# Decay attention with a SoLU layer on one core: GpSimd centres z by adding the negated mean, and the order of all operations is searched anew

## The chip, the cores and the metric

The kernel runs on one core of a Trainium2 chip. The metric is the device time of one execution in microseconds (us); lower is better. A core has five engines that run side by side, each working through its own instructions in order: TensorE (PE in the profile, its weight loads PEld), VectorE (DVE), ScalarE (ACT), GpSimd (POOL) and SyncE (SP), which issues the DMAs here. They wait for one another on semaphores.

## The reference, cut to what matters

```python
# attention: q, k, v (8, 8, 576, 64), f (8, 8, 576)
scores = scale * np.matmul(q, k.transpose(0, 1, 3, 2))
cum = np.cumsum(np.log(np.clip(f, 0.0001, 1.0)), axis=-1)
scores = np.where(causal, -1000000000.0, scores + cum[:, :, :, None] - cum[:, :, None, :])
attn = np.exp(scores - max(scores)) ; attn = attn / (sum(attn) + 1e-09)
x = (attn @ v)  # as 4608 tokens x 512
# layer: w_in (512, 1024), w_out (1024, 512)
h = x @ w_in
e = np.exp(h - h_max)
solu = h * e / (np.sum(e, axis=-1, keepdims=True) + 1e-09)
mu = np.mean(solu, axis=-1, keepdims=True)
var = np.mean((solu - mu) ** 2, axis=-1, keepdims=True)
ln = (solu - mu) / np.sqrt(var + 1e-06) * g_ln
return ln @ w_out
```

The last lines are what the change touches: each token's 1024 values are centred by their mean and scaled by their deviation before the second product.

## The kernel before, in words

Every fp32 operand of a product is split into a high and a low fp16 part, and each product is three fp16 matmuls (high x high, low x high, high x low). The kernel works in two interleaved streams.

*Attention.* 32 pairs of heads (8 batches x 4 pairs). For a pair, `split_qk` and `split_v` make the fp16 parts: GpSimd the high part (L489, L750), VectorE the low one (L741, L751). `score_products` (TensorE, L778 and L780) fills PSUM banks, VectorE masks and takes the maximum (L800), ScalarE takes the exponential (L805), GpSimd adds 1e-9 to the sums (L811) and VectorE inverts them (L812). P is scaled and split into fp16 by ScalarE or GpSimd (L487, L489) and VectorE (L827), transposed by DMA on SP's queue (L496), and multiplied by v (TensorE, L849); ScalarE and VectorE split the result into x (L858, L859).

*Layers.* 36 groups of 128 tokens, `layer(n)`. TensorE makes h in PSUM (L879 to L881). VectorE takes its maximum (L892, L893), ScalarE the exponential (L895), VectorE weighs it by h and sums (L899). GpSimd turns the sums into factors: `sums` (L903 to L905), where L905 makes `s[:, 4:5]`, the mean. ScalarE squares and sums the deviations (L909), and GpSimd's `deviation` (L913, L914) makes `s[:, 7:8]`, the reciprocal deviation. Then z is made from `et`, which holds the weighed values:

- for layers 3 to 32 (30 of them), L919 on GpSimd centres `et` in place, with mean and deviation as operands taken per partition; ScalarE copies it to fp16 (L487, tile z), GpSimd subtracts to get the low part (L923), and both are transposed by one DMA;
- for layers 0 to 2, 33 and 34, L928 on GpSimd writes the centred z in fp32, and TensorE transposes it (L939), with splits by ScalarE (L942) and VectorE (L943);
- for layer 35, L928 runs on VectorE in two halves.

TensorE makes the output of the layer in a PSUM bank (L951 to L953), ScalarE scales it (L983) and SP stores it.

The order of the work is made by a planner when the program is built. Every operation is entered with an engine, a cost in ns, its dependences, and a rank from the list `RANK` (3720 entries), which takes the place of the due time given with it. `Plan.schedule` then simulates the five engines by those costs and takes, on each engine, the lowest rank among the operations that are ready or nearly so. What comes out is a fixed order of instructions per engine (SP's DMA queue included) and the PSUM bank of each product. On the chip each engine keeps this order, whatever the real durations are. The planner's costs that matter here: 1165 ns for the centring at L919 and 1220 at L928 on GpSimd, 650 for `deviation`, 950 for `sums`, 1350 for the weighing, and 150 (`SWITCH`) whenever TensorE goes from one form of matmul to another. Where the planner sees TensorE idle before 140 us and after 690 us of its own time, it puts matmuls on a constant (L1075) that compute nothing.

Of the kernel before, what the change touches and what calls it, by code (L numbers as in the profile page):

```python
# [15 lines left out]
ALU = mybir.AluOpType  # L16
# [3 lines left out]
B, H, S, D = 8, 8, 576, 64  # L20
NPAIR = H // 2
NT, DM, DFF = B * S, 512, 1024
# [15 lines left out]
PE, ACT, DVE, POOL, SP = range(5)  # L38
# [23 lines left out]
SWITCH = ((0.0, 150.0, 0.0, 150.0), (150.0, 0.0, 150.0, 150.0), (0.0, 150.0, 0.0, 150.0), (150.0, 150.0, 150.0, 0.0))  # L62
# [11 lines left out]
class Plan:  # L74
# [125 lines left out]
DUE = dict(split=16.32, v=-48.52, S=((10.42, -178.61), (-76.5, -43.51), (-17.84, 9.11), (-33.83, -25.65), (-338.51, -196.13)), T=(109.24, 340.52, -82.29, -127.23, -60.67), V=(-7.63, 56.62))  # L200
EARLY = dict(split=362.28, v=-97.59, S=((-411.23, -149.52), (-71.89, 66.22), (-245.09, -190.59), (-76.46, 23.88), (22.21, -234.26)), T=(-72.02, -152.54, -5.6, -408.25, -113.91), V=(-252.88, -30.84))
LATE = dict(split=98.43, v=174.22, S=((-17.11, -184.22), (262.31, 198.88), (-309.42, 7.37), (-32.81, 315.39), (118.17, -135.55)), T=(-189.94, -447.79, -346.65, 143.53, -213.83), V=(45.44, 171.68))
PAIR = 19.22
C_OUT = -1186.29
C_LOAD = -414.2
START = 55.12
HALF = ((-18.23, 31.03), (-177.88, -65.59))
FINAL = ((612.38, -120.01), (574.97, -91.39))
W_IN = (-124.17, -35.6)
W_OUT = (114.81, 6.76)  # L210
WI_SCALE = (-281.95, 282.86)
VDUE = (271.75, 1385.66, -57.91)
QDUE = (148.6, 265.36, 191.09)
W_SCALE = 469.26
W_DMA = (340.69, 250.23)
AT_P = ((-81.67, 61.16, 60.23, 192.14, 69.55, -100.01, -98.02, 300.72), (-145.79, 357.44, 17.6, 61.32, 14.21, -14.54, -172.11, 33.3), (141.14, 169.03, -125.66, -194.75, -29.29, 69.66, -241.42, -50.24), (-161.17, 125.62, -280.73, -119.52, -307.95, 75.0, -172.56, 168.03), (53.4, 12.94, 59.05, -81.54, -65.95, -187.09, -104.95, -79.9), (57.9, 109.17, -65.96, 150.72, -25.16, -82.81, 36.45, -8.16), (70.77, 133.63, 12.76, -7.44, 191.47, -123.42, 272.56, -18.37), (21.29, 142.9, 37.73, 313.97, 43.82, -67.44, 60.97, -521.28), (174.0, 168.03, 225.82, 361.17, 52.24, 81.8, 314.01, -241.37), (74.44, -51.03, 294.31, 305.07, 2.7, 84.27, -129.0, -33.77), (119.59, -15.83, -61.33, 18.64, -123.18, -57.85, 111.65, -131.16), (68.91, -122.6, 34.58, -83.09, 83.91, 102.57, -179.31, 35.06), (190.89, 62.67, 9.66, 34.42, -143.48, -186.72, -16.07, -334.64), (15.13, -57.55, -54.74, -107.42, -116.07, -287.16, -220.22, -252.55), (332.62, -121.34, -54.52, -218.21, -55.32, -30.68, 22.54, 170.65), (-57.32, -255.01, -70.11, -225.0, -2.07, 17.04, -35.42, -47.88), (-27.85, 64.37, -177.02, -84.25, -204.85, 158.78, 40.98, -78.34), (64.44, 76.4, -166.26, -216.1, 128.23, 164.74, 20.38, -202.94), (-67.41, -175.96, -53.63, -139.42, -116.31, 92.32, -98.02, 23.06), (-34.62, -99.73, -34.72, -107.59, -43.28, 25.95, -59.91, 21.41), (-197.38, 99.1, 77.91, -87.49, -101.39, -44.62, -10.73, -432.6), (76.35, -52.66, -146.11, -57.9, -32.02, 20.35, -9.36, -41.36), (284.63, -33.64, -59.72, -35.36, 13.16, -50.56, 111.1, -209.08), (-170.21, 17.59, 22.48, -18.35, -145.72, 148.72, -38.82, -153.28), (117.16, -118.25, -147.0, -84.5, -216.07, -97.89, 17.93, -21.37), (19.52, 129.07, 84.34, 107.44, 28.14, 165.39, 116.59, -105.27), (35.5, 2.96, -74.65, -119.02, -111.77, 33.07, -159.25, 73.15), (-137.99, -76.09, 98.87, -83.71, 39.3, 53.58, 88.01, 118.53), (-73.29, -23.24, -279.13, -8.79, 152.09, -154.48, -73.79, 73.15), (116.11, 4.31, -44.41, 87.07, -47.65, 327.91, 111.04, 63.74), (119.79, 166.23, -85.34, -98.88, -1.08, 185.35, -23.71, 210.62), (-10.74, 3.74, 66.08, 111.57, -99.16, -276.89, -13.72, -336.84))
STEPS = (-4.08, -26.31, -34.38, -3.27, -7.29)
XSTEP = (-40.34, 35.34)
AT_L = ((-254.45, -131.81, -28.71, 162.54), (129.2, 133.0, -66.4, -97.75), (0.16, 51.2, -66.64, -216.93), (27.84, 199.95, 50.97, 33.36), (-31.05, -140.35, 257.32, 37.01), (9.35, -73.92, -30.24, -139.45), (75.8, 16.59, 6.38, -28.89), (-31.5, -16.15, 5.27, 35.3), (-99.98, -146.39, -116.22, -14.35), (-0.39, -65.93, -16.48, 55.16), (36.33, -12.74, -45.85, 6.72), (-41.24, -55.87, -46.44, 40.3), (7.03, 41.84, -82.9, -173.0), (-93.41, -117.32, -38.75, -26.07), (-47.53, 52.85, 15.16, -87.73), (10.27, 20.72, 230.99, 138.02), (10.21, 46.78, 185.1, 145.78), (56.68, -116.87, -221.71, 140.0), (85.62, -125.98, -15.49, 39.67), (-161.28, 65.64, -134.56, -113.34), (28.35, 25.51, -55.67, 64.12), (-33.19, -41.91, 47.28, -41.75), (-92.58, 111.35, 0.14, 39.65), (-45.33, 21.88, 91.63, 134.69), (228.29, -26.11, -19.26, -117.38), (-117.29, 36.02, -120.02, 67.48), (237.85, 58.15, -36.94, -123.12), (-185.8, -87.16, -219.01, 97.21), (42.34, 163.22, 98.63, 248.34), (-34.9, -42.96, 198.6, -38.06), (203.64, 142.69, 74.54, -92.81), (-202.74, 75.26, -28.07, -252.01), (-86.6, -144.99, 45.93, 151.88), (218.16, 25.2, 97.92, 313.38), (308.03, -15.23, -72.11, -87.35), (3.75, -320.4, 375.02, -12.8))
FIRST = 89.94  # L220
STAGES = (62.88, 1.27, -19.84, 26.95, 22.69)

RANK = (
# [151 lines left out]
def tile_kernel(ctx: ExitStack, tc: tile.TileContext, qk, v, f, w_in, w_out, g_ln, out):  # L375
# [104 lines left out]
    def engine(e):  # L480
        return {DVE: nc.vector, POOL: nc.gpsimd}[e]
# [640 lines left out]
```

## Time and profile before

| what | value |
|---|---|
| median of 3 runs | 766.3 us (763.89 to 771.79) |
| profiled execution | 766.7 us, span 764.7 us |
| granted TensorE clock, mean | 0.971 |
| centring on GpSimd (L919), 30 passes | 115.7 us, 3787 ns median |
| the same to fp32 z (L928), 5 passes | 19.0 us, 3787 ns median |
| low part of z (L923), 30 passes | 64.8 us, 2130 ns median |

Rows of the profile name a line of the kernel, an engine, and tiles as output<-inputs with their shapes. Numbers such as 3781/3787/4849 are the least, the median and the greatest duration in ns, followed by the start of the first and the last one in us. A row of waits reads "waiting instruction <- what it waited for: us in total, times, longest us". In a row of order in time, a bracket at the end gives the engine's idle time before the instruction and what ended it.

### The profile page before, as it was taken

What the parts mean: (1) busy time and instruction counts of PE and PEld (TensorE: products, weight loads), DVE (VectorE), ACT (ScalarE), POOL (GpSimd) and SP (SyncE); (2) the same over time, 40 slices, a digit from 0 to 9 for tenths busy, and PEclk for the clock granted to TensorE, in tenths of its full rate; (3) what the DMA queues carried; (4) which work ended last, traced back from release to release, by engine and by line L of the source; (5) the groups of instructions that cost most, each with busy time, mean ns of one, the idle gap of its engine ahead of it and who ended that gap; (6) DMA issues with size and microseconds to landing.
All of it is one profiled execution on the core that took longest, in us unless ns stands there. A gap on an engine that the chain in (4) does not pass through costs nothing. (4 is left out here: it accounts for less than half of the span.)

```text
span 764.7 us, 18744 instructions
## 1 busy us (share of the span) xinstructions
PE 684.8 (90%) x6937; PEld 389.3 (51%) x6937; DVE 577.5 (76%) x1701; ACT 533.8 (70%) x1334; POOL 460.1 (60%) x599
## 2 busy tenths in 40 slices
PE   9999987885979998997899898998898997979998
PEld 8877654543444444444444454444454544445445
DVE  4798888987886988778878787997888865575422
ACT  7788947778777876776667776987767667553433
POOL 4330386456269467587388776787587585373750
PEclk9999999997889999999999999999999999998999
DMA  8699157867957798997779866998494577458321
GB/s 355 232 257 196 41 90 192 153 172 154 197 139 158 162 177 171 178 158 140 152 121 225 166 130 140 216 180 174 108 162 108 119 114 134 77 111 144 82 55 42
DMA packets 284241, 116.33 MB, mean 152 GB/s; under 512 B 269814, under 2 KB 270262, under 8 KB 283126
## 3 DMA queue, kind: packets, MB, share of 16 engines
q1 hardware_dynamic: 284150, 115.14, 70.8%
q8 instruction: 54, 0.88, 0.5%
q14 instruction: 37, 0.30, 0.1%
HBM read 38.12 MB, written 9.88 MB: 63 GB/s over the span
## 5 line engine op out<-in xcount | busy, mean ns | idle before, releaser
L805 ACT ACTIVATE ps<-ps,nm 128x192 f32<-128x192 f32 (+3 forms) x256 | 113.8, 445 | 32.8 <-DVE nm L800 29.6
L780 PE MATMUL ps<-qk 64*128 64x288 f16 (+4 forms) x1152 | 98.1, 281 | 25.6 <-DVE wo_p L827 12.2
L919 POOL TENSOR_SCALAR e<-e,st 128x1024 f32<-128x1024 f32 x30 | 115.7, 3857 | 2.9
L951 PE MATMUL ps<-wo_f,zz 128*128 128x512 f16 x280 | 107.7, 385 | 10.8 <-DVE p16s L827 4.7
L849 PE MATMUL ps<-t_p,v 128*64 128x128 f16 (+1 forms) x2880 | 98.6, 226 | 21.0 <-DVE p16s L827 10.0
L879 PE MATMUL hps<-wi_h,x_h 128*128 128x512 f16 x288 | 111.5, 387 | 5.7 <-DVE e L899 5.7
L811 POOL TENSOR_SCALAR sm<-sm 128x2 f32<-128x2 f32 (+1 forms) x128 | 38.4, 300 | 126.7 <-ACT ps L805 97.8
L800 DVE CUSTOM_DVE_ANT_0 ps<-ps,mask 128x192 f32<-128x192 f32 (+3 forms) x256 | 102.9, 444 | 11.1 <-PE ps L778 10.6
L880 PE MATMUL hps<-wi_l,x_h 128*128 128x512 f16 x288 | 111.1, 386 | 0.0
L881 PE MATMUL hps<-wi_h,x_l 128*128 128x512 f16 x288 | 110.7, 384 | 0.0
L849 PEld LDWEIGHTS <-v 128*64 128x64 f16 x2880 | 87.2, 115 | 43.0 <-issue 39.2
L952 PE MATMUL ps<-wo_f,zz 128*128 128x512 f16 x280 | 107.2, 383 | 0.0
L953 PE MATMUL ps<-wo_f,zz 128*128 128x512 f16 x280 | 106.9, 382 | 0.0
L487 ACT ACTIVATE p16s<-ps,ri 64x64 f16<-64x64 f32 (+2 forms) x192 | 68.8, 416 | 19.4 <-DVE ri L812 17.2
L827 DVE SCALAR_TENSOR_TENSOR p16s<-ps,ri,p16s 128x192 f16<-128x192 f32 (+2 forms) x192 | 71.2, 406 | 14.3 <-ACT p16s L487 13.5
L780 PEld LDWEIGHTS <-qk 64*128 64x128 f16 x1152 | 44.9, 95 | 68.0 <-issue 52.5
L923 POOL TENSOR_TENSOR z<-e,z 128x1024 f16<-128x1024 f32 x30 | 64.8, 2161 | 17.4 <-ACT z L487 16.8
L487 ACT ACTIVATE z<-e 128x1024 f16<-128x1024 f32 x30 | 31.7, 1057 | 60.8 <-POOL e L919 60.7
L1075 PEld LDWEIGHTS <-ident 128*128 128x128 bf16 x673 | 65.0, 99 | 14.6 <-issue 4.5
L1075 PE MATMUL hps<-ident 128*128 128x256 bf16 x560 | 65.9, 277 | 1.3 <-POOL ident masks.py:199 1.3
L741 DVE SCALAR_TENSOR_TENSOR qk<-raws,scale,qk 128x576 f16<-128x576 f32 x64 | 58.0, 917 | 8.6 <-POOL qk L489 8.4
L489 POOL TENSOR_SCALAR qk<-raws,scale 128x576 f16<-128x576 f32 x64 | 50.0, 790 | 21.6 <-DVE scale L638 9.0
(171 smaller groups left out, 1348.2 us busy)
## 6 DMA issues: line engine op xcount, KB each, us to landing
raws<-in_qk_dram SPq DMA_DIRECT2D x32, 576.0 KB, 7.0
vraw<-in_v_dram SPq DMA_DIRECT2D x8, 1280.0 KB
out_dram<-y SPq DMA_DIRECT2D x35, 256.0 KB, 3.5
wo_raw<-in_w_in_dram SPq DMA_DIRECT2D x4, 1024.0 KB
vraw<-in_w_out_dram SPq DMA_DIRECT2D x2, 1024.0 KB, 6.7
t_raw<-in_w_out_dram SPq DMA_DIRECT2D x2, 1024.0 KB, 7.7
t_p<-p16s SPq DMA_TRANSPOSE x96, 3.2
t_p<-wo_p SPq DMA_TRANSPOSE x64, 5.3
```

The costliest lines, as they stand in the source:

```text
L780: nc.tensor.matmul(dst, x[row(h), 0, q0:q0 + P], y[row(h), 1, cols], start=(n == 0), stop=False)
L800: op(DVE, R_NS[i] if n == 0 else 442, at[i][h] + STEPS[0], lambda i=i, h=h, n=n, a=a, e=e, x=x, m0=m0: nc.vector.tensor_tensor_reduce(home ...
L805: op(ACT, E_NS[i], at[i][h] + STEPS[1], lambda i=i, h=h, x=x: nc.scalar.activation(home(i, h), home(i, h), AF.Exp, bias=x, scale=-1.0, acc ...
L849: nc.tensor.matmul(o[row(h), a:a + n], v16[m][:, x, 2 * j + h], t[:, y, i + j if h else i - j], start=(j == 0 and c == 0), stop=(j == i an ...
L879: nc.tensor.matmul(hps[:, sl], x_h, wi_h[:, c, sl], start=(c == 0), stop=False)
L880: nc.tensor.matmul(hps[:, sl], x_h, wi_l[:, c, sl], start=False, stop=False)
L881: nc.tensor.matmul(hps[:, sl], x_l, wi_h[:, c, sl], start=False, stop=(c == NCC - 1))
L919: op(c_eng, {POOL: 1165, DVE: 690}[c_eng], at, lambda: engine(c_eng).tensor_scalar(et, et, s[:, 4:5], s[:, 7:8], ALU.subtract, ALU.mult), ...
L951: nc.tensor.matmul(o, zz[:, a, 0, j], wo(0, k), start=(k == 0), stop=False)
L952: nc.tensor.matmul(o, zz[:, a, 0, j], wo(1, k), start=False, stop=False)
L953: nc.tensor.matmul(o, zz[:, a, 1, j], wo(0, k), start=False, stop=(k == NFC - 1))
L1075: nc.tensor.matmul(dst[:, :256], blank[:, :P], blank, start=True, stop=True)
```

## The change

The mean is stored with a negative sign, and the centring adds it in place of subtracting it, in all three places:

```diff
-            nc.gpsimd.tensor_scalar(s[:, 4:5], s[:, 3:4], 1.0 / DFF, 1.0, ALU.mult, ALU.mult)
+            nc.gpsimd.tensor_scalar(s[:, 4:5], s[:, 3:4], -1.0 / DFF, 1.0, ALU.mult, ALU.mult)
...
-            op(c_eng, {POOL: 1165, DVE: 690}[c_eng], at, lambda: engine(c_eng).tensor_scalar(et, et, s[:, 4:5], s[:, 7:8], ALU.subtract, ALU.mult),
+            op(c_eng, {POOL: 1165, DVE: 690}[c_eng], at, lambda: engine(c_eng).tensor_scalar(et, et, s[:, 4:5], s[:, 7:8], ALU.add, ALU.mult),
...
-                    zt[:, sl], et[:, sl], s[:, 4:5], s[:, 7:8], ALU.subtract, ALU.mult), [ek, ("st4", n % 2), ("st7", n % 2)], [zk], clear=[zk_, (*zk_, "l")], port=c_eng == DVE)
+                    zt[:, sl], et[:, sl], s[:, 4:5], s[:, 7:8], ALU.add, ALU.mult), [ek, ("st4", n % 2), ("st7", n % 2)], [zk], clear=[zk_, (*zk_, "l")], port=c_eng == DVE)
```

Three of the planner's costs change, those of the centring stay:

```diff
-SWITCH = ((0.0, 150.0, 0.0, 150.0), (150.0, 0.0, 150.0, 150.0), (0.0, 150.0, 0.0, 150.0), (150.0, 150.0, 150.0, 0.0))
+SWITCH = ((0.0, 120.0, 0.0, 120.0), (120.0, 0.0, 120.0, 120.0), (0.0, 120.0, 0.0, 120.0), (120.0, 120.0, 120.0, 0.0))
...
-        op(DVE, 1350, at, weigh, [("h",)], [("st3", n % 2), ek])
+        op(DVE, 1220, at, weigh, [("h",)], [("st3", n % 2), ek])
...
-        op(POOL, 650, at, deviation, [("st5", n % 2), ("st4", n % 2)], [("st7", n % 2)])
+        op(POOL, 1030, at, deviation, [("st5", n % 2), ("st4", n % 2)], [("st7", n % 2)])
```

All entries of `RANK` are new: the same 3720 ranks, dealt out again. Half of the operations move by 12 places or fewer, the one that moves most by 248. The tables of due times (`DUE`, `EARLY`, `LATE`, `AT_P`, `AT_L` and the constants beside them) change too; the rank takes their place in the planner.

More of the change, by code (lines that the diff above doesn't have):

```diff
@@ L196, in spare @@
                 a = min(y for spans in self.held.values() for _, y in spans if y > a)
-DUE = dict(split=16.32, v=-48.52, S=((10.42, -178.61), (-76.5, -43.51), (-17.84, 9.11), (-33.83, -25.65), (-338.51, -196.13)), T=(109.24, 340.52, -82.29, -127.23, -60.67), V=(-7.63, 56.62))
-EARLY = dict(split=362.28, v=-97.59, S=((-411.23, -149.52), (-71.89, 66.22), (-245.09, -190.59), (-76.46, 23.88), (22.21, -234.26)), T=(-72.02, -152.54, -5.6, -408.25, -113.91), V=(-252.88, -30.84))
-LATE = dict(split=98.43, v=174.22, S=((-17.11, -184.22), (262.31, 198.88), (-309.42, 7.37), (-32.81, 315.39), (118.17, -135.55)), T=(-189.94, -447.79, -346.65, 143.53, -213.83), V=(45.44, 171.68))
@@ L203 @@
[L203 to L216, printed above, removed]
@@ L217 @@
-STEPS = (-4.08, -26.31, -34.38, -3.27, -7.29)
-XSTEP = (-40.34, 35.34)
-AT_L = ((-254.45, -131.81, -28.71, 162.54), (129.2, 133.0, -66.4, -97.75), (0.16, 51.2, -66.64, -216.93), (27.84, 199.95, 50.97, 33.36), (-31.05, -140.35, 257.32, 37.01), (9.35, -73.92, -30.24, -139.45), (75.8, 16.59, 6.38, -28.89), (-31.5, -16.15, 5.27, 35.3), (-99.98, -146.39, -116.22, -14.35), (-0.39, -65.93, -16.48, 55.16), (36.33, -12.74, -45.85, 6.72), (-41.24, -55.87, -46.44, 40.3), (7.03, 41.84, -82.9, -173.0), (-93.41, -117.32, -38.75, -26.07), (-47.53, 52.85, 15.16, -87.73), (10.27, 20.72, 230.99, 138.02), (10.21, 46.78, 185.1, 145.78), (56.68, -116.87, -221.71, 140.0), (85.62, -125.98, -15.49, 39.67), (-161.28, 65.64, -134.56, -113.34), (28.35, 25.51, -55.67, 64.12), (-33.19, -41.91, 47.28, -41.75), (-92.58, 111.35, 0.14, 39.65), (-45.33, 21.88, 91.63, 134.69), (228.29, -26.11, -19.26, -117.38), (-117.29, 36.02, -120.02, 67.48), (237.85, 58.15, -36.94, -123.12), (-185.8, -87.16, -219.01, 97.21), (42.34, 163.22, 98.63, 248.34), (-34.9, -42.96, 198.6, -38.06), (203.64, 142.69, 74.54, -92.81), (-202.74, 75.26, -28.07, -252.01), (-86.6, -144.99, 45.93, 151.88), (218.16, 25.2, 97.92, 313.38), (308.03, -15.23, -72.11, -87.35), (3.75, -320.4, 375.02, -12.8))
@@ L220 @@
-FIRST = 89.94
-STAGES = (62.88, 1.27, -19.84, 26.95, 22.69)
-RANK = (
[148 rows of a table removed]
+DUE = dict(split=26.66, v=-44.32, S=((17.02, -148.33), (-64.42, -44.95), (-28.43, 12.9), (-42.71, -39.48), (-325.28, -188.8)), T=(64.32, 327.76, -59.68, -127.5, -47.39), V=(-7.74, 31.59))
+EARLY = dict(split=332.95, v=-57.66, S=((-372.38, -152.17), (-57.66, 30.21), (-183.97, -159.95), (-60.8, 76.81), (-22.89, -163.49)), T=(-33.47, -7.72, -4.8, -396.65, -124.51), V=(-142.51, -66.42))
+LATE = dict(split=81.6, v=174.09, S=((-5.61, -234.66), (198.9, 135.47), (-236.01, 0.28), (28.81, 328.08), (107.14, -163.85)), T=(-115.44, -433.88, -336.19, 140.0, -108.98), V=(-5.0, 176.08))
@@ new lines @@
+PAIR = 18.5
+C_OUT = -1212.08
+C_LOAD = -650.15
+START = 54.54
+HALF = ((53.14, -17.86), (-150.28, -79.69))
+FINAL = ((625.5, -127.51), (555.3, -109.92))
+W_IN = (-77.74, 17.6)
+W_OUT = (120.75, 49.66)
+WI_SCALE = (-540.34, 296.98)
+VDUE = (387.16, 1315.13, -62.36)
+QDUE = (217.4, 372.26, 220.19)
+W_SCALE = 360.35
+W_DMA = (193.38, 344.79)
+AT_P = ((25.12, 95.62, 42.16, 214.24, 43.75, -38.59, -81.69, 295.75), (-140.06, 200.42, -1.28, 29.81, 26.59, -27.74, -186.97, 33.02), (151.37, 195.04, -155.18, -161.83, -33.15, 38.49, -268.94, -41.72), (-188.64, 177.31, -240.94, -78.79, -249.47, 134.65, -191.84, 84.33), (78.5, -23.93, -9.71, -105.86, -48.06, -187.29, -125.06, -49.3), (-10.91, 90.41, -28.2, 131.1, -90.03, -116.36, 52.65, -32.0), (44.39, 170.77, 20.96, 2.3, 190.15, -182.08, 257.81, -7.06), (-32.76, 95.23, 28.91, 293.82, 41.19, 24.48, 59.59, -494.43), (127.94, 195.94, 193.63, 316.21, 45.94, 34.03, 326.37, -137.96), (-6.2, -97.44, 217.38, 248.58, 19.46, 70.9, -92.14, -25.49), (121.42, 60.05, -22.1, -11.23, -121.91, -2.29, 132.03, -111.33), (32.66, -138.46, 79.08, -42.76, 99.42, 117.62, -152.76, 38.35), (196.54, 55.31, -3.46, 61.33, -136.97, -285.2, 55.2, -274.07), (-45.42, -1.66, -57.0, -59.94, -99.97, -248.68, -156.0, -313.23), (386.4, -82.49, -41.1, -212.17, -144.74, -39.5, 22.85, 130.81), (-59.36, -348.05, -101.26, -223.62, 19.02, 26.31, -42.36, -47.72), (-53.2, 38.85, -130.81, -77.55, -124.95, 87.25, 61.74, -77.39), (114.44, 126.78, -97.19, -98.45, 91.01, 128.76, -17.2, -157.42), (-74.01, -169.16, -72.96, -154.95, -82.3, 139.28, -79.89, 85.69), (-87.64, -117.78, -17.76, -80.71, -59.89, 74.78, -92.64, 11.91), (-196.75, 132.15, 30.41, -51.27, -120.99, -41.33, 27.23, -384.56), (66.74, -9.87, -155.12, -45.59, 21.27, -46.64, -19.77, -64.26), (219.6, -103.86, -40.04, -49.66, 3.96, -44.52, 101.91, -242.53), (-63.49, 57.48, -24.49, -14.19, -128.28, 170.9, 2.34, -130.24), (93.61, -63.91, -141.55, -155.61, -202.75, -159.35, -7.93, -81.72), (79.19, 96.47, 65.92, 79.02, 8.96, 103.79, 87.29, -56.01), (-8.82, -16.91, -90.94, -101.98, -75.29, 29.98, -161.2, 71.04), (-79.85, -11.88, 92.61, -122.03, 39.2, 26.82, 68.15, 86.35), (-88.98, 13.18, -253.98, -65.27, 149.91, -88.3, -118.94, 32.32), (72.19, 40.68, -36.67, 67.31, -98.0, 300.39, 62.89, 60.29), (60.8, 60.72, -11.49, -88.29, -25.19, 218.25, -56.5, 259.62), (-33.59, -92.07, -1.6, 70.4, -107.46, -180.71, -26.23, -366.15))
@@ new lines @@
+STEPS = (-13.54, -40.97, -32.65, -12.55, -1.17)
+XSTEP = (-48.05, 27.24)
+AT_L = ((-258.51, -153.97, -4.33, 210.08), (168.98, 33.84, -93.21, -51.12), (32.61, -13.28, -48.9, -230.65), (48.25, 146.46, 106.43, 61.35), (-18.07, -102.64, 250.55, 25.26), (14.53, -125.12, -103.17, -137.93), (59.87, 17.33, -16.45, -24.6), (-13.03, 4.49, -11.5, 31.96), (-82.02, -122.21, -77.18, -69.46), (12.94, -129.84, 27.02, 95.75), (13.55, -48.5, -33.52, 54.59), (-40.69, -58.19, -29.71, 37.27), (-11.38, 90.54, -113.02, -167.06), (-86.13, -190.38, -20.6, -37.79), (-58.04, 67.22, 2.8, -78.32), (-21.6, -17.64, 158.76, 195.63), (39.93, 53.75, 187.44, 72.57), (30.57, -76.49, -176.86, 102.4), (42.66, -86.16, -90.45, 5.33), (-166.78, 76.34, -171.01, -107.9), (8.98, 20.69, -122.96, 47.93), (28.81, -87.76, 51.94, 4.38), (-65.2, 124.63, 10.44, 45.83), (-67.84, 42.79, 1.34, 127.92), (196.85, -32.98, -29.79, -105.47), (-3.71, 66.12, -135.39, 49.55), (293.04, 41.3, -52.7, -73.8), (-191.9, -103.36, -215.11, 86.7), (33.1, 177.79, 112.22, 202.83), (-63.26, -61.66, 197.66, 3.01), (228.21, 123.93, 42.91, -155.2), (-207.74, 97.91, -8.48, -230.7), (-100.03, -169.01, -25.92, 144.94), (255.73, 66.83, 96.45, 251.62), (304.45, -36.26, -91.98, -113.8), (-18.0, -237.35, 323.2, 58.7))
@@ L374, in tile_kernel @@
+FIRST = 88.9
+STAGES = (39.55, 3.04, -33.03, 23.93, 18.38)
+RANK = (
[148 rows of a table added]
 @with_exitstack
```

296 rows, old and new, of the table RANK are left out of this document.

## The prediction

> **What bounds the kernel now.** I read the page first (busy shares, the 40 slices), then the stretches of time, then the chain of waits followed back from the end, then GpSimd's own groups and waits.
>
> ```profile
> span 764.7 us, 18744 instructions
> PE 684.8 (90%) x6937; PEld 389.3 (51%) x6937; DVE 577.5 (76%) x1701; ACT 533.8 (70%) x1334; POOL 460.1 (60%) x599
> PEclk9999999997889999999999999999999999998999
> ```
>
> TensorE is the fullest engine, and GpSimd is busy for only 60% of the span. A cheaper GpSimd instruction can therefore shorten the kernel only where another engine stands waiting for it. The stretches say how much TensorE leaves free (columns: TensorE, weight loads, VectorE, ScalarE, GpSimd, then granted clock, DMA share, GB/s).
>
> ```profile
> 0.00:160.00 160.00, 147.65 (x1609) 106.21 (x1609) 130.79 (x391) 123.63 (x296) 71.81 (x121) 1.00 0.72 186
> 160.00:720.00 560.00, 495.90 (x5058) 260.37 (x5059) 433.29 (x1290) 393.74 (x1012) 373.81 (x461) 0.96 0.75 150
> 720.00:764.00 44.00, 41.27 (x271) 22.74 (x269) 13.42 (x21) 16.43 (x27) 14.53 (x19) 1.00 0.18 52
> 160.00:200.00 40.00, 27.99 (x334) 16.51 (x335) 31.80 (x93) 27.69 (x73) 20.84 (x28) 0.83 0.85 181
> 480.00:520.00 40.00, 38.49 (x371) 19.35 (x370) 36.71 (x105) 33.88 (x89) 30.55 (x39) 1.00 0.97 190
> ```
>
> In the long middle, 160 to 720 us, TensorE is busy 495.9 of 560 us, which is 35.4 of every 40; 64.1 us are idle. One window there reaches 38.5 of 40, another only 28.0. In the last 44 us only 2.7 us are idle. What the change can win lies in the middle, and no engine is full there, so it is waiting that costs.
>
> ```profile
> by line: POOL e L919 4.4%; issue 4.0%; DVE wo_p L827 1.4%; ACT junk L909 1.4%; PE ps L951 1.1%; PE ps L953 1.1%; PE ps L952 1.1%; ACT e L895 1.1%; DVE st L892 1.1%; DVE e L899 1.0%; PE ps L849 0.9%; DVE qk L741 0.8%; POOL z L923 0.8%; POOL
> 514.14 0.09 DVE ri L812
> 546.43 3.80 POOL e L919
> 728.76 3.80 POOL z L928
> ```
>
> The chain could be followed back only to 514.14 us, so its shares, which are of the whole span, describe the last 250.6 us. In these the centring at L919 is its largest line: 4.4% of 764.7 is 33.6 us, or 13% of the stretch that the chain covers.
>
> ```profile
> ACT z L487 <- POOL e L919: 60.7, 25, 7.2
> POOL sm L811 <- ACT ps L805: 97.8, 40, 10.5
> DVE ri L812 <- POOL sm L811: 42.9, 28, 5.8
> ACT p16s L487 <- DVE ri L812: 17.2, 17, 3.2
> PE ps L780 <- DVE wo_p L827: 12.2, 9, 3.9
> ```
>
> These rows of the list of waits (us in total, times, longest) show how a slow GpSimd reaches TensorE. ScalarE stands still for the centred tile 25 times, 60.7 us in all (2.43 us each); and what GpSimd has queued behind the centring, the softmax sums of L811, keeps VectorE's reciprocal, then the splits of P, then the PSUM banks that TensorE wants. The same in order of time on GpSimd:
>
> ```profile
> 664.05 3.79 POOL L919 TENSOR_SCALAR e<-e,st 128x1024 f32<-128x1024 f32 x1
> 667.93 0.19 POOL L811 TENSOR_SCALAR sm<-sm 128x2 f32<-128x2 f32 x1
> 668.43 1.46 POOL L489 TENSOR_SCALAR wo_p<-p,ri 128x576 f16<-128x576 f32 x2 [0.31 <-DVE ri L812]
> ```
>
> **The change part by part.** *The duration of the centring.*
>
> ```profile
> L919 POOL TENSOR_SCALAR e<-e,st x30: 3781/3787/4849, 176.9 to 715.3; 128x1024 f32<-128x1024 f32 x30
> L928 POOL TENSOR_SCALAR z<-e,st x5: 3781/3787/3802, 101.7 to 738.9; 128x1024 f32<-128x1024 f32 x5
> L489 POOL TENSOR_SCALAR wo_f<-wo_f,sg x4: 688/690/691, 87.6 to 90.0; 128x512 f16<-128x512 f32 x4
> L750 POOL TENSOR_SCALAR v<-vraw,scale x32: 792/801/1416, 41.7 to 647.5; 128x640 f16<-128x640 f32 x32
> L923 POOL TENSOR_TENSOR z<-e,z x30: 2121/2130/2617, 185.7 to 721.3; 128x1024 f16<-128x1024 f32 x30
> L666 POOL TENSOR_SCALAR unscale<-unscale,scale_wo x8: 333/342/981, 87.3 to 566.2; 128x1 f32<-128x1 f32 x8
> ```
>
> The trace has no add-then-multiply of this size, so its price is bounded. The same engine multiplies twice over 512 elements in 690 ns and over 640 in 801: 111 ns for 128 more, 0.867 ns each, with 246 ns fixed. For 1024 that is 801 + 384 x 0.867 = 1134 ns, the low end. The centring as it stands, 3787 ns, is the high end: then nothing is gained. In between lies the subtraction of two whole tensors, 2130 ns. That row also says that subtracting as such is not what costs 3787: with twice the input it is faster. What is particular to L919 is the pair subtract-then-multiply, with both operands taken per partition. L666 takes two such operands too, and over one element costs 342 ns, so the second operand brings no large fixed cost; whether it costs per element no row shows. I take 1134 ns, since every other one-tensor pass of this engine lies on that line, and keep 3787 as a rival. A pass then saves 3787 - 1134 = 2653 ns: 30 x 2.65 = 79.6 us at L919 and 5 x 2.65 = 13.3 us at L928, 93 us of GpSimd's time in all.
>
> [...]
>
> *What the engine change reaches in the middle.* Ceiling by the chain: after 514 us it passes through 11 of the 12 L919 and one of the two L928; 12 x 2.65 = 31.8 us. The same 12 of 14 applied to the 18 L919 before it gives 15.4 x 2.65 = 41 us more, some 73 us, if nothing else were nearly as late. A lot else is: TensorE has only 64.1 us of idle time there to give, and the waits quoted above end on many different things. Two estimates below the ceiling. First, ScalarE's 60.7 us for L919: 25 waits shortened by at most 2.65 us each, of which I count 50 as going. ScalarE is idle 560 - 393.7 = 166 us in that stretch, so 30% of its idle time goes; 30% of TensorE's 64.1 is 19 us. Second, if TensorE's share rises halfway from its mean of 35.4 to its best window's 38.5, to 36.95 of 40, its 495.9 us take 537 us in place of 560: 23 us. I take 21 us, with 0 and 64 as the ends.
>
> *The untransposed tiles* (L928).
>
> ```profile
> PE ps L939 <- POOL z L928: 7.0, 4, 2.5
> PE hps L879 <- DVE e L899: 5.7, 9, 1.7
> ```
>
> TensorE waited for these tiles directly, 7.0 us in four times, none longer than 2.5 us, which the 2.65 us saved would cover; other matmuls and transposes stand ready behind some of these waits, so I take 3 us, of at most 7.
>
> *Contention.* VectorE's instructions on SBUF tiles are lengthened beside GpSimd's passes. The rows show its qk split beside the slow centring (which ran from 561.40 for 3.81 us) and beside two fast GpSimd passes; undisturbed its median is 812 ns.
>
> ```profile
> 562.09 1.12 DVE L741 SCALAR_TENSOR_TENSOR qk<-raws,scale,qk 128x576 f16<-128x576 f32 x1
> 487.52 1.47 POOL L489 TENSOR_SCALAR qk<-raws,scale 128x576 f16<-128x576 f32 x2
> 488.30 1.29 DVE L741 SCALAR_TENSOR_TENSOR qk<-raws,scale,qk 128x576 f16<-128x576 f32 x1
> L741 DVE SCALAR_TENSOR_TENSOR qk<-raws,scale,qk x64: 784/812/2667, 28.0 to 617.4; 128x576 f16<-128x576 f32 x64
> ```
>
> Beside the fast passes VectorE loses 0.48 us, beside the slow one 0.31. If a third of the 35 passes meets such an instruction, 12 x 0.48 = 6 us of VectorE's time are lost, against 0.31 each now; most of it lies in VectorE's own idle time. I take 2 us lost, between 0 and 6.
>
> *The sign.* The third instruction of the sums (L905) multiplies by -1/1024 in place of 1/1024: the same instruction and cost, nothing to hide. Only the centring reads its result. On VectorE the last layer adds in place of subtracting:
>
> ```profile
> L928 DVE TENSOR_SCALAR z<-e,st x2: 543/544/546, 752.4 to 752.8; 128x512 f32<-128x512 f32 x2
> ```
>
> That is 544 ns for 512 elements, already quicker than GpSimd's 690 for a double multiply, so I cost this at nothing; even at GpSimd's saving in proportion, 70% of 1.09 us, it would be under a microsecond at the end.
>
> *The new order.* All operations get new ranks, the planner charges 120 ns for a change of matmul form (before 150), 1220 for the weighing (1350) and 1030 for the deviation (650). It charged 1165 and 1220 ns for the centring, and still does; on the chip that was 2.6 us too little, 35 times, so the present order has every centring late by its own book. The ranks move by few places (half of the 3720 by 12 or fewer), so no stage moves. What the order is worth by itself no row can show. Its bound: one wrongly placed operation costs a wait like those seen (1.7 to 7.2 us at the engines), and a few are lost or won. The deviation's new cost is near the chip's:
>
> ```profile
> 545.40 0.27 POOL L913 TENSOR_SCALAR st<-st 128x1 f32<-128x1 f32 x1 [1.68 <-ACT junk L909]
> 545.75 0.57 POOL L914 TENSOR_TENSOR st<-st,mhalf 128x1 f32<-128x1 f32 x1
> 546.43 3.79 POOL L919 TENSOR_SCALAR e<-e,st 128x1024 f32<-128x1024 f32 x1
> ```
>
> From the first of these to the centring pass 1.03 us. An order that is made with truer costs should fit somewhat better: 4 us won, between 15 won and 10 lost. The DMA transposes of z are issued earlier by what the centring saves, and in SP's queue they move with their ranks; they cost nothing as long as the transposes of P ahead of them are not late, and the 15 and 10 cover the case that they are.
>
> **Sum.** The profiled execution took 766.7 us for a span of 764.7, and the median of the three runs is 766.3, so the two agree. 766.7 - 21 - 3 + 2 - 4 = 740.7, say 741 us.
>
> **The rivals.**
> 1. *The pass doesn't get faster.* For it: 3787 ns may come from two per-partition operands in one pass, a form that remains. Against it: GpSimd's one-tensor passes all run at 0.87 ns per element, and a two-tensor subtraction at 2.1. Then only the order differs: 766.7 - 4 = 763, from 752 to 777.
> 2. *Fast, but hidden.* TensorE's named waits end mostly on VectorE (12.2 us at the score products), which is 76% busy. If ScalarE merely moves its idle time to the next wait for VectorE, there remain L928 and the order: about 762.
> 3. *The whole chain shortens.* If the centring was nearly always the last thing awaited, two thirds of the 73 us come: 766.7 - 49 = 718.
> 4. *Slower: the granted clock falls.* After the first 160 us, where TensorE is 92% busy, the rows above show 0.83 at 160 to 200 us; in the middle the mean is 0.96. If a fuller TensorE is granted less throughout the middle, its 495.9 us grow as 0.96/clock. The saving of 26 us is eaten at 0.96 x 495.9 / 521.9 = 0.91, and from there on it is slower: at 0.88 it takes 45 us more and the kernel 766.7 - 26 + 45 = 786. Against it: the fullest window, 480 to 520, was granted 1.00.
>
> **How the numbers follow.** The forecast has 0.62, rival 1 0.12, rival 2 0.08, rival 3 0.12, rival 4 0.06. A measurement of this kernel tells about 1% from no change, 7.7 us. Faster by more than that: 0.61 + 0.12 + a little of rivals 1 and 2 (0.02 each) = 0.77; within it 0.01 + 0.07 + 0.06 = 0.14; slower 0.03 + 0.06 = 0.09. The forecast's own range is 722 to 756. The range for all goes to 712, below rival 3's number, and to 768, which takes in rival 2 and most of rival 1, and leaves out rival 4.
>
> **What would show it.** Right: L919 and L928 at 1.1 to 1.2 us on GpSimd, GpSimd's busy time near 370 us, ScalarE's wait for L919 under 15 us, L919 gone from the head of the chain, and TensorE near 37 of 40 in the middle. L919 still at 3.8 us makes it wrong at the first step (rival 1); a fast L919 with ScalarE's idle time unchanged and renamed, at the second (rival 2); a mean clock under 0.92 in the middle, rival 4. A time under 722 us says that I undervalued the chain, or the order.

## The result, and the profile after

The changed kernel takes 704.45 us (703.16 to 706.36), the kernel before 766.41 us in the same comparison: a ratio of 0.919 (0.913 to 0.924), 62 us less. The forecast was 741 us, with 712 as its lower end. The sign was right and the size was not.

The page of the kernel after, answering to the lines shown of before:

```profile
span 702.0 us, 18805 instructions
PE 669.3 (95%) x6964; PEld 382.9 (55%) x6964; DVE 577.0 (82%) x1701; ACT 530.8 (76%) x1334; POOL 371.2 (53%) x599
PEclk9999999999999999999999999999999999999999
```

GpSimd lost 89 us of busy time, near the 93 worked out. TensorE is busy for 95% of the span in place of 90%, and its mean granted clock is 0.998 in place of 0.971.

The same kernel's passes, its long middle, and its waits:

```profile
L919 POOL TENSOR_SCALAR e<-e,st x30: 1187/1195/2204, 173.5 to 655.3; 128x1024 f32<-128x1024 f32 x30
L928 POOL TENSOR_SCALAR z<-e,st x5: 1193/1194/1209, 107.0 to 679.9; 128x1024 f32<-128x1024 f32 x5
```

```profile
160.00:658.00 498.00, 481.10 (x5094) 253.09 (x5094) 433.72 (x1306) 394.72 (x1023) 296.85 (x466) 1.00 0.85 167
```

```profile
ACT z L487 <- POOL e L919: 8.6, 10, 1.9
DVE ri L812 <- POOL sm L811: 12.8, 18, 1.6
PE ps L849 <- DMA t_p<-wo_p: 3.1, 4, 1.4
PE hps L879 <- DVE e L899: 2.7, 5, 0.9
PE ps L780 <- DVE wo_p L827: 0.9, 1, 0.9
```

The pass fell from 3787 to 1195 ns. In the middle TensorE is busy 481.1 of 498 us, which is 38.6 of every 40, above the best single window of before. ScalarE's wait for the centring fell from 60.7 to 8.6 us and VectorE's for the softmax sums from 42.9 to 12.8. The score products' wait for VectorE's splits of P fell from 12.2 us to 0.9.

The chain of waits followed back from the end now leads with TensorE itself:

```profile
by line: PE ps L951 3.1%; PE hps L879 3.0%; PE ps L952 3.0%; PE ps L953 3.0%; PE ps L849 2.9%; PE hps L880 2.8%; PE hps L881 2.8%; PE ps L780 2.1%; issue 1.3%; ACT ps L805 1.3%; DMA t_p<-p16s 1.0%; DVE ps L800 0.7%; DMA zz<-z 0.6%; DVE p16s
```

The signs that the prediction named for "right" are all there, but TensorE is busy for 38.6 of 40 in the middle where it said 37: the mechanism is there, and the size of what it brings was wrong.

### The profile page after: what moved, and what is told of

The parts are those of the page before. It is cut to its first block, busy times and chain, and to the rows that moved or that the text cites. A ratio compares the mean times of both kernels' runs of the same rounds, so it can differ in the third digit from the quotient of the medians.

```text
span 702.0 us, 18805 instructions
## 1 busy us (share of the span) xinstructions
PE 669.3 (95%) x6964; PEld 382.9 (55%) x6964; DVE 577.0 (82%) x1701; ACT 530.8 (76%) x1334; POOL 371.2 (53%) x599
## 5 line engine op out<-in xcount | busy, mean ns | idle before, releaser
L805 ACT ACTIVATE ps<-ps,nm 128x320 f32<-128x320 f32 (+3 forms) x256 | 113.9, 446 | 20.1 <-DVE nm L800 17.4
L800 DVE CUSTOM_DVE_ANT_0 ps<-ps,mask 128x320 f32<-128x320 f32 (+3 forms) x256 | 101.7, 447 | 6.9 <-PE ps L778 6.7
L849 PE MATMUL ps<-t_p,v 128*64 128x128 f16 (+1 forms) x2880 | 94.6, 219 | 11.1 <-DMA t_p<-wo_p 3.1
L849 PEld LDWEIGHTS <-v 128*64 128x64 f16 x2880 | 82.4, 110 | 37.0 <-issue 31.8
L780 PE MATMUL ps<-qk 64*128 64x288 f16 (+4 forms) x1152 | 93.2, 276 | 4.2 <-DVE x_l L859 1.2
L923 POOL TENSOR_TENSOR z<-e,z 128x1024 f16<-128x1024 f32 x30 | 67.5, 2248 | 16.5 <-ACT z L487 16.1
L487 ACT ACTIVATE p16s<-ps,ri 128x320 f16<-128x320 f32 (+2 forms) x192 | 68.2, 419 | 2.9 <-DVE ri L812 1.3
L805 ACT ACTIVATE p<-p,nm 128x576 f32<-128x576 f32 x64 | 49.0, 768 | 19.1 <-DVE nm L800 18.9
L489 POOL TENSOR_SCALAR wo_p<-p,ri 128x576 f16<-128x576 f32 x64 | 54.9, 864 | 12.9 <-DVE ri L812 8.2
```

The lines of the kernel that those rows point to most:

```text
L489: (nc.vector if eng == DVE else nc.gpsimd).tensor_scalar(now(out_), now(in_), scale, 1.0, ALU.mult, ALU.mult)
L780: nc.tensor.matmul(dst, x[row(h), 0, q0:q0 + P], y[row(h), 1, cols], start=(n == 0), stop=False)
L800: op(DVE, R_NS[i] if n == 0 else 442, at[i][h] + STEPS[0], lambda i=i, h=h, n=n, a=a, e=e, x=x, m0=m0: nc.vector.tensor_tensor_reduce(home ...
L805: op(ACT, E_NS[i], at[i][h] + STEPS[1], lambda i=i, h=h, x=x: nc.scalar.activation(home(i, h), home(i, h), AF.Exp, bias=x, scale=-1.0, acc ...
L849: nc.tensor.matmul(o[row(h), a:a + n], v16[m][:, x, 2 * j + h], t[:, y, i + j if h else i - j], start=(j == 0 and c == 0), stop=(j == i an ...
```

## The experiments

Every time below is a median; times of before differ a little from set to set (766.4 to 768.6), so ratios go by the runs of the same set, and a difference between two sets is sure to some 2 us only.

**The parts alone.** First the add without the new order, then the new order without the add.

```diff
  RANK, SWITCH and costs of before
-  ... 1.0 / DFF, 1.0 ...   ... ALU.subtract, ALU.mult ...
+  ... -1.0 / DFF, 1.0 ...  ... ALU.add, ALU.mult ...
```

> The order, ranks and planner's costs of before; only the sign and the add are new. Theory A (the faster pass carries most of the 62 us won): 704 to 725 us, TensorE idle in the long middle falls from 64 to under 30 us. Theory B (the new order carries more than half of it): 735 to 750 us, as the forecast's terms without its order term give (766.7 - 21 - 3 + 2 = 745). Theory C (the order pays only with the fast pass, and the reverse): 730 to 750 us here, and nothing won with the order alone.

```diff
  RANK, SWITCH and costs of after
-  ... -1.0 / DFF, 1.0 ...  ... ALU.add, ALU.mult ...
+  ... 1.0 / DFF, 1.0 ...   ... ALU.subtract, ALU.mult ...
```

> The new ranks and planner's costs, but GpSimd subtracts the mean as before. L919 back at 3.79 us. Theory A: 755 to 775 us, as before. Theory B: under 735 us. Theory C: 755 us or more, with the clock granted below 0.98 again and ScalarE waiting some 50 us or more for L919.

The add in the old order: 710.7 us, a ratio of 0.926 (0.923 to 0.929), 56.6 us less. The new order with the subtraction: 763.3 us, 0.994 (0.992 to 0.996), 4 us less. Theory A holds: the pass carries nine tenths, and on top of it the order brings some 6 us (the two kernels with the add were run in different sets; their ratios, 0.926 and 0.919, have intervals that just touch). Theory C, that the order pays only with the fast pass, falls with the 710.7. The page of the add in the old order, and its long middle:

```profile
span 707.0 us, 18744 instructions
PE 668.2 (95%) x6937; PEld 383.5 (54%) x6937; DVE 573.1 (81%) x1701; ACT 532.5 (75%) x1334; POOL 368.6 (52%) x599
PEclk9999999999899999999999999999999999999999
160.00:665.00 505.00, 477.80 (x5046) 252.66 (x5045) 425.38 (x1283) 390.09 (x1003) 293.19 (x456) 0.99 0.84 165
```

TensorE is idle there for 27.2 us, where it was 64.1 before.

**The order's two halves.** New ranks with the old costs of the planner, and old ranks with the new costs, both with the add.

```diff
  after.py
- SWITCH 120, weigh 1220, deviation 1030
+ SWITCH 150, weigh 1350, deviation 650
```

> The add and the new ranks, but the planner charges 150, 1350 and 650 ns as before for the change of form, the weighing and the deviation. If what the order is worth lies in the ranks: within 1% of the changed kernel's 704 us. If it lies in the three costs: 5 us or more above it.

```diff
  before.py with the add
- SWITCH 150, weigh 1350, deviation 650
+ SWITCH 120, weigh 1220, deviation 1030
```

> The add with the old ranks and the three new costs (120, 1220 and 1030 ns). If ranks and costs only fit together, as the 745 us of the new ranks with the old costs say: 725 to 750 us. If truer costs help any ranks: 710 us or less.

745.1 us and 756.8 us: 41 us above the changed kernel, and 46 above the old order with the add. Both mixes lose most of what the pass wins, so each set of ranks goes with its own costs here; mixes nearer to either order were not run. Truer costs alone are no gain.

**What made the pass slow.** GpSimd's pass by itself, in thirteen forms, four times each, on a core with nothing else to do (e and s as in the kernel, a and b per-partition operands):

```python
g.tensor_scalar(z, e, a, b, ALU.subtract, ALU.mult)   # L24
g.tensor_scalar(z, e, a, b, ALU.add, ALU.mult)        # L26; L28 mult, mult; L30 mult, add; L32 mult, subtract
g.tensor_scalar(z, e, 0.25, 0.5, ALU.subtract, ALU.mult)  # L34; L36 add, mult; L38 mult, mult
g.tensor_scalar(z, e, a, None, ALU.subtract)          # L40; L42 add
g.tensor_scalar(z[:, :512], e[:, :512], a, b, ALU.subtract, ALU.mult)  # L44; L46 add, mult; L48 add, mult in place
```

> Computes no attention: it only runs GpSimd's one-tensor pass over 128 x 1024 fp32, four times in each form, on an otherwise idle core. If the pair subtract-then-multiply is what is slow: 3.79 us for it with per-partition operands and with constants alike, 1.13 to 1.20 us for add-then-multiply, multiply-multiply and multiply-add. If two per-partition operands made it slow (first rival of the prediction): add-then-multiply with them at 3.8 us too. If any subtraction is slow: the lone subtraction and multiply-then-subtract at 3 us or more as well.

Its groups on GpSimd (busy us, mean ns of one):

```profile
L32 POOL TENSOR_SCALAR z<-e,s 128x1024 f32<-128x1024 f32 x4 | 15.1, 3781 | 0.4
L24 POOL TENSOR_SCALAR z<-e,s 128x1024 f32<-128x1024 f32 x4 | 15.1, 3779 | 4.3 <-DMA s<-in_q_dram 4.0
L34 POOL TENSOR_SCALAR z<-e 128x1024 f32<-128x1024 f32 x4 | 14.5, 3631 | 0.3
L42 POOL TENSOR_SCALAR z<-e,s 128x1024 f32<-128x1024 f32 x4 | 11.4, 2843 | 0.4
L40 POOL TENSOR_SCALAR z<-e,s 128x1024 f32<-128x1024 f32 x4 | 11.4, 2842 | 0.4
L44 POOL TENSOR_SCALAR z<-e,s 128x512 f32<-128x512 f32 x4 | 8.3, 2072 | 0.4
L30 POOL TENSOR_SCALAR z<-e,s 128x1024 f32<-128x1024 f32 x4 | 4.8, 1194 | 0.4
L26 POOL TENSOR_SCALAR z<-e,s 128x1024 f32<-128x1024 f32 x4 | 4.8, 1194 | 0.4
L36 POOL TENSOR_SCALAR z<-e 128x1024 f32<-128x1024 f32 x4 | 4.2, 1044 | 0.3
L46 POOL TENSOR_SCALAR z<-e,s 128x512 f32<-128x512 f32 x4 | 3.1, 767 | 0.4
```

The three pairs with a subtraction take 3.6 to 3.8 us, with the subtraction first or second, with constants or not; the pairs of add and multiply that were run take 1.0 to 1.2 (L28, two multiplications, and L48, in place, 1194 ns too). Two per-partition operands cost 150 ns more than constants (1194 against 1044), so the first rival's reason is gone. A lone operation, add or subtract, is slow as well, 2842 ns: what is fast is a form, two operations out of add and multiply. Why the other forms are slow no run shows.

**Where the lateness reaches TensorE.** In the old order with the add, passes over a small tile that nothing else uses are put into GpSimd's queue; one over 324 elements takes 1.30 us. They give back the lateness with the fast centring, at a chosen place. They are subtract-then-multiply passes themselves, so that few elements take long.

```diff
  e1 (old order, add); dump is a tile of 324 elements a partition
+ nc.gpsimd.tensor_scalar(dump, dump, 0.0, 1.0, ALU.subtract, ALU.mult)   # twice: 2.6 us
  nc.gpsimd.tensor_scalar(et, et, s[:, 4:5], s[:, 7:8], ALU.add, ALU.mult)
```

> Old order with the add (710.7 us), and in front of each of the 30 centrings at L919 two more GpSimd passes of some 1.3 us each over a tile that nothing else uses, so that the centred tile and all that GpSimd has queued behind it come 2.6 us later, as with the subtraction. If it is the lateness that costs: 755 to 768 us, with 30 to 45 us of half clock. If something else about the slow pass costs (its reads of SBUF beside VectorE's): under 740 us.

The same with one pass, and with one and a part of another:

> One such pass of 1.3 us ahead of each centring: half the lateness. If the cost goes with the lateness in proportion: 735 to 742 us, halfway between 710.7 and the kernel with two. If the order swallows a first part of it, or the half clock comes only with longer stalls: 715 to 730 us.

> One pass of 1.3 us and one of some 0.6 ahead of each centring, 2.0 us in all. On a straight line from 722.6 (1.3 us) to 763.7 (2.6 us): 744 us. If there is a step at which the order has no slack left: under 730 or over 755.

Then two passes behind the centring (`et` first, then `dump` twice), and two right behind and right ahead of L923, the low part of z:

> The same two passes, but right behind the centring: the centred tile is there in time for ScalarE, while GpSimd's queue behind it (softmax sums, splits, the low part of z) is as late as with the subtraction. Theory Q (it is GpSimd's queue that reaches TensorE): within 10 us of the kernel with the passes ahead. Theory L (it is ScalarE standing for the centred tile, 61 us of waits before): 730 us or less.

> Old order with the add (710.7 us), and the two GpSimd passes of 1.3 us right behind L923, which makes the low part of z: the layer's own chain (centring, copy, low part, DMA transpose, second product) is on time, and only what GpSimd has queued behind L923 is late. Theory Q (the attention's work in GpSimd's queue is the link to TensorE): 740 us or more. Theory Z (the layer's own chain is): 728 us or less.

> The two passes right ahead of L923: centring and ScalarE's copy on time, and so is what GpSimd's order has between L919 and L923; the low part of z and all that follows are late. If it is only what lies between L919 and L923 that counts: 725 us or less. If lateness in GpSimd's queue costs wherever it is put: 740 to 765 us, like the passes right behind the centring (754).

| where | late by | time | above 710.7 |
|---|---|---|---|
| ahead of L919 | 2.6 us | 763.7 us | 53 |
| ahead of L919 | 2.0 us | 744.5 us | 34 |
| ahead of L919 | 1.3 us | 722.6 us | 12 |
| behind L919 | 2.6 us | 754.4 us | 44 |
| ahead of L923 | 2.6 us | 742.2 us | 32 |
| behind L923 | 2.6 us | 748.7 us | 38 |

The centring is fast here, and the old time comes back all the same (53 of 56.6 us). The passes put in are slow ones and read SBUF too, so by itself the run does not tell lateness from a contention with VectorE. VectorE's busy time does: 573.1 us with the add alone, 578.0 with two passes ahead, 577.5 before. 5 us more on an engine that is idle for a quarter of the span are too few for the 53. The time that TensorE spent at half clock was (1 - 0.966) x 763.4 / 0.5 = 52 us, an estimate from the mean clock that takes the reduced clock as 0.50, as the kernel before was granted it (from 311.68 to 315.09 us, for one). It was more than the 30 to 45 expected.

The shape is bent: up to 1.3 us a layer each us of lateness costs 9 us of time, beyond that 32. And lateness costs at every place, though not the same: 32 to 53 us. With the passes behind the centring, ScalarE has its tile in time, and with them behind L923 the layer's own chain has all that GpSimd makes for it; 44 and 38 us are lost all the same. Theory Q holds, theories L and Z fall: it is what stands behind in GpSimd's queue. The attention's instructions and the next layers' own both stand there, and no run parts these two. The wait of VectorE for the softmax sums, 12.5 us with the add alone, moves with the lateness (line numbers are two higher where two lines were added), here ahead by 1.3 us, behind L919 and ahead of it by 2.6:

```profile
DVE ri L814 <- POOL sm L813: 24.9, 24, 3.2
```

```profile
DVE ri L814 <- POOL sm L813: 44.0, 28, 3.8
ACT z L489 <- POOL e L922: 10.4, 8, 4.6
```

```profile
DVE ri L814 <- POOL sm L813: 44.5, 28, 5.9
ACT z L489 <- POOL e L924: 59.9, 25, 6.7
```

The second row of the middle fence is the point: ScalarE waits only 10.4 us for the centred tile there, against 59.9 with the passes ahead, and the kernel still takes 754 us.

**The softmax sums taken out of the queue.**

```diff
- ... lambda: nc.gpsimd.tensor_scalar(sums, sums, 1.0e-9, 1.0 / P_UP, ALU.add, ALU.mult)
+ ... lambda: nc.vector.tensor_scalar(sums, sums, 1.0e-9, 1.0 / P_UP, ALU.add, ALU.mult)
```

> The kernel before, with the slow subtraction and its order, but the 128 additions of 1e-9 to the softmax sums (L811) are issued on VectorE at the same places, so that they no longer stand behind the centring on GpSimd. If the softmax sums are the link from GpSimd's queue to TensorE: 740 us or less, and half clock under 25 us. If what is late is rather the splits of P and of q, k and v that GpSimd makes, or the layer's own chain: 755 us or more.

> The changed kernel with L811 on VectorE at the same places: 12.8 us of VectorE's waits for GpSimd go, but VectorE, busy 82%, gets 128 instructions more (some 20 us). If the rest of GpSimd's lateness still reaches TensorE: 2 to 8 us faster than 704. If TensorE is now the bound, with 22 us idle in all: within 1%, or slower by VectorE's extra work.

772.4 us in the kernel before (1.008, 1.004 to 1.011) and 721.0 in the changed one. VectorE's 42.9 us of waits for the sums went, and nothing was won.

```profile
PE 684.5 (89%) x6937; PEld 390.1 (51%) x6937; DVE 605.0 (79%) x1829; ACT 535.4 (70%) x1334; POOL 426.5 (56%) x471
```

In the kernel before, VectorE got 27.5 us more to do (605.0 against 577.5). In the changed kernel the move costs 17 us, in the one before 5; so the sums account for perhaps 12 of the 56, if these two costs may be set against each other. Which other instruction of the queue carries the rest is not settled: the splits of P, q, k and v, the low part of z and the next layers' sums are all late together.

**Keeping TensorE occupied.**

```diff
- FILLED = ((0.0, 140.0, 1.2), (690.0, 1000.0, 0.8))
+ FILLED = ((0.0, 140.0, 1.2), (140.0, 1000.0, 0.8))
```

> The kernel before, subtraction and all, with the planner also filling the idle time that it foresees between 140 and 690 us with matmuls that compute nothing (63 more of them). If keeping TensorE occupied keeps its clock: half clock falls below the 44 us of before and the time by 2 to 10 us. The planner foresees only part of the stalls, since it charges 1165 ns for the centring; if its 63 lie elsewhere than the stalls, no change within 1%.

784.7 us, 16 more than before, at a mean clock of 0.967, and no verdict on whether a fuller TensorE would have kept its clock: the planner's own clock model reads the same table, so the order of all engines moved too, and no ranks were searched for it.

## Why the prediction was wrong, point by point

*The pass* was right: 1134 ns foretold, 1195 measured, 2.59 us saved a pass; the rate of the other passes held, and the missing 61 ns lie within the 150 of two per-partition operands. What I read out of L923, that subtracting as such is not what is slow, holds for two whole tensors only (2130 ns): every pass over 128 x 1024 of one tensor with a subtraction was slow (2842 to 3781 ns), and so was an add by itself (2843). That one operation feeds another does not tell the forms apart: an add feeding a multiplication costs 1194 ns, a multiplication feeding a multiplication the same, a subtraction feeding a multiplication 3779.

*The middle* is the step that failed. The prediction took 21 us there, from ScalarE's 60.7 us of waits for L919 and from a share of TensorE's idle time. With the 3 for L928 and the 2 lost to contention the faster pass was to bring 22; alone it brought 56.6. Two things were wrong in the term: what it counted, and what it left out.

First, the wait that I counted is not the path. ScalarE's is the longest that ends on the centring, but with GpSimd's queue equally late, 50 us more of it (59.9 against 10.4) cost only 9 us of time (763.7 against 754.4). GpSimd's queue behind the centring is what reaches TensorE, and I had quoted it without pricing it. The chain ceiling of 73 us, which counts every visit of the chain to L919 in full, was nearer than the halving that I preferred to it.

Second, the sum had no term for TensorE's clock, and the fourth rival had it with the wrong sign. Between before and the add in the old order, with the same 6937 matmuls, the span fell 57.7 us: TensorE's idle time from 79.9 to 38.8, and its busy time from 684.8 to 668.2. The first part, 41 us (37 of it in the long middle), is by itself nearly twice what the term gave. The second, 16.6 us, is clock for the most part:

```profile
core 0: 764.7 us, clock 0.971
```

```profile
core 0: 707.0 us, clock 0.990
```

(1 - 0.971) x 764.7 = 22.2 us and (1 - 0.990) x 707.0 = 7.1: 15.1 us less, an estimate that takes TensorE as busy whenever its clock was low. A stall with half clock right behind it, in the kernel before, as stretches and then as TensorE's instructions in order of time:

```profile
629.00:632.60 3.60, 3.60 (x17) 1.47 (x16) 0.00 (x0) 2.36 (x8) 2.43 (x2) 1.00 0.94 183
632.60:635.90 3.30, 0.13 (x3) 0.07 (x3) 2.08 (x6) 2.76 (x10) 1.26 (x3) 1.00 0.64 125
635.90:639.30 3.40, 3.40 (x45) 2.33 (x45) 2.96 (x10) 3.11 (x9) 0.73 (x3) 0.51 1.32 197
639.40:642.80 3.40, 3.40 (x65) 2.12 (x64) 1.21 (x5) 1.89 (x6) 3.19 (x3) 1.00 0.62 128
```

```profile
635.83 0.88 PE L780 MATMUL ps<-qk 64*128 64x320 f16 x5 [3.17 <-DVE p16s L827]
638.82 0.61 PE L951 MATMUL ps<-wo_f,zz 128*128 128x512 f16 x1
639.50 0.38 PE L953 MATMUL ps<-wo_f,zz 128*128 128x512 f16 x1
```

TensorE waits 3.17 us, is then granted half its clock for 3.4 us (0.51 in the third stretch), in which a matmul of 0.38 us takes 0.61, and has its full clock again. The kernel before has eight stretches granted 0.50, of 3.41, 6.83 or 13.65 us, and all of them start on one grid of 3.41 us: at 181.98, 222.94, 311.68, 376.53, 475.52, 554.03, 635.95 and 687.15 us. A wait need not be that long: one of 1.78 us, up to 310.19, was followed by half clock from 311.68 to 315.09, while one of 2.91 us, up to 347.53, lay across a line of the grid (345.81) and the clock stayed at 1.00 (345.81 to 349.22). What decides whether half clock follows a wait no run shows.

The fourth rival had a fuller TensorE granted less, and these three kernels show the reverse: in the long middle TensorE was busy for 89% before, 95% with the add and 97% in the changed kernel, and was granted 0.96, 0.99 and 1.00. The dip to 0.83 at 160 to 200 us, which I read as a price for the full start, comes with that window's own stalls: TensorE was idle there for 12 us, with waits of up to 3.35.

*L928*: not measured apart. Two passes ahead of L919 alone, with L928 fast, leave the kernel 0.995 (0.992 to 0.997) of before, some 4 us, which fits the 3 taken.

*Contention* had the wrong sign, at a small size: VectorE's busy time fell with the fast pass, from 577.5 to 573.1 us in the old order and from 582.1 to 577.0 in the new one. Nor was every split beside a slow pass lengthened: in the kernel before, three qk splits that ran wholly beside L928 or L919 (from 103.95, 117.06 and 330.47 us) took 0.80 to 0.81 us.

*The order*: 4 us taken, 4 measured on the slow pass and 6 on the fast one. The bounds of 15 and 10 held for the order as it is; with ranks and costs mixed it lost 41 and 46.

*The rivals*: the whole chain shortening (718 us) came nearest, and its 0.12 should have been more, since the planner's 1165 ns for a pass of 3787 is a misfit that sits in every layer. That the old order works so well with the add because the pass now takes what its planner charged is argued, not shown; that an order loses 41 to 46 us by a change of its costs, and 53 by 2.6 us a layer of lateness, is shown.

## What to carry to other kernels

In a kernel whose engines run a fixed order, price a slow instruction by everything queued behind it on its engine, and not by the one wait that the list puts beside it; here the ceiling from the chain of waits (73 us) was nearer to the 56.6 than the share of idle time (21). When a change removes stalls of TensorE, look at its granted clock as well: here some 15 of the 57.7 us, by the estimate above, came with it. When a duration that the order was planned with turns out wrong by a factor, look first for a form of the instruction that has the planned duration, and change the planner's costs together with a new search: alone they lost 46 us here.

## What the runs showed of the hardware that was not expected

- On GpSimd the form of a one-tensor pass over 128 x 1024 fp32 sets its time: 1194 ns for two operations out of add and multiply with per-partition operands, 3780 ns with a subtraction in the pair (3631 with constants), 2842 ns for a single add or subtract. An add followed by a multiplication is thus quicker than the add by itself.
- The rate of the slow pair, (3779 - 2072) / 512 = 3.33 ns per element, against (1194 - 767) / 512 = 0.83 for the fast one.
- An idle stretch of TensorE of 3.17 us was followed by 3.4 us at half clock, and so was one of 1.78 us; one of 2.91 us across a line of the 3.41 us grid was not. The mean clock was 0.971 before and 0.998 after, for the same products (and 27 more matmuls on the constant at the start).
